# New prices for a planner that orders every engine, and one more wait

## The chip, the cores and the metric

The kernel runs on one core of a Trainium2 chip. The core has five engines that work side by side, each through its own list of instructions, and that meet only at semaphores: TensorE (PE, matrix products into PSUM), VectorE (DVE), ScalarE (ACT, here mostly exponentials), GpSimd (POOL) and SyncE (SP, which issues the DMAs). The metric is the time of one execution on the device in microseconds; of several runs the median is taken. "PEld" in the profile is TensorE's loading of weights.

## The reference

The inputs are x (2048 tokens of 512 values), wqkv (512 x 1536), wo (512 x 512), w_gate and w_up (512 x 1376), w_down (1376 x 512) and gate_w (512). Three things are computed and mixed:

```python
g = sigmoid((x * gate_w).sum(-1, keepdims=True))
# attention, 32 heads of 16
q, k, v = (x @ wqkv) split into heads
p = softmax(q @ k.T * 16 ** -0.5)
a = (p @ v) @ wo
# gated bilinear layer
b = ((x @ w_gate) * (x @ w_up)) @ w_down
return g * a + (1 - g) * b
```

The costly part is the softmax: 32 heads x 2048 x 2048 exponentials.

## The kernel before, in words

**Tiling.** The queries are cut into four chunks of 512 tokens (c), the heads into four groups of eight (b), and a group into two halves of four heads (p = 0, 1). One (c, b, p) is a stage m, of which there are 32. Inside a stage the keys are cut into 16 tiles of 128 (kt). A **unit** is one head of a stage with one key tile: scores of 128 keys x 512 queries, which fill one of the eight PSUM banks. There are 32 x 16 x 4 = 2048 units.

**What happens to a unit.** TensorE computes the scores (line 1224) as four small matmuls of 64 x 32 in one of its two row groups; the two row groups run side by side, and such a set of four is a *pack*. The exponential is then taken in one of two ways. ScalarE takes two neighbouring banks in one activation and writes two cells of PT (line 1319, a *pair*). Or VectorE takes one bank and forms the exponent's bits by an addition into int16 (line 1383, a *pass*); such a unit needs three further copies of its cell, shifted by a constant, which VectorE (line 1336) or GpSimd (line 1335) makes, and in the product with V all four cells are used, against four scaled copies of V. The product with V (PV, line 1669) is again made in packs, one for each row group, into one bank for the stage. A unit of ScalarE thus costs TensorE two PV matmuls (one in each row group), a unit of VectorE eight.

**The end of a stage.** The function `norm` handles it. VectorE copies the stage's bank to the raw buffer `oraw` (line 1608). DMAs then take the denominators out (`den`), VectorE forms the reciprocal (line 1543), further DMAs write it to memory and read it back spread over the partitions (`rb`), and GpSimd multiplies the raw output of both halves of a pair of stages by it (line 1586). For the second half, four DMAs first move its rows within `oraw`. `oraw` and `rb` are used again by the next pair of stages.

**Fills.** Between the scores and the PV packs TensorE works through a list of other products in packs (line 559): projections of q, k, v, the gate, the bilinear layer, and the output projection. VectorE empties their banks. The weights of the bilinear layer are loaded by SyncE into a ring of five slots.

**What sets the order.** Everything is ordered by a planner that runs when the program is built. It plays the five engines in time, each action with a price: `a_cad(n)` for a ScalarE activation of n banks, `d_cad` and `d_fast` for VectorE, `p_cad` for GpSimd, `PEC` = 0.2155 us for a pack and `PEL` = 0.437 us until its result is seen, and for each DMA a time to issue (the argument `cost`) and a time to land. `A_LAT`, `D_LAT`, `P_LAT` are the times until others see an end. Whenever an engine is free, its policy picks what it does next from what is ready in planned time: `pe_policy` tries a score first, then PV and fills in an order that depends on the stage. In `score`, a unit goes to ScalarE if its planned backlog is below 0.6 us (`TLO`), or up to 1.6 (`TA`) if VectorE can't take it, and to VectorE if VectorE's planned load is below 1.2 us, or 0.6 when a unit is already queued for it (`DTH`, `DTH2`), and if enough cells and a bank are free. ScalarE's units use banks 0 to 3, everything else banks 4 to 7. The order so found is written out for each engine with the semaphore waits that the data need. On the chip each engine then runs its list in that order as fast as its waits let it; the planned times play no further part.

Of the kernel before, what the change touches and what calls it, by code (L numbers as in the profile page):

```python
# [125 lines left out]

class _Res:

    __slots__ = ("at", "rel")

    def __init__(self):
        self.at = 0.0
# [51 lines left out]
def _build(nc, A_x, A_wqkv, A_wo, W_gate, W_up, W_down, gate_w, out):  # L184
# [10 lines left out]
    NB = 4  # L195
# [13 lines left out]
    NW = 5  # L209
# [42 lines left out]
    XC = 0.26  # L252
    AW = 0.3
    KF = 0
    GM = (2, 1)

    def a_cad(n):
        return 0.0505 + 0.4267 * n

    A_LAT = 0.17  # L260

    def d_cad(n):
        return 0.068 + n / 960.0
# [15 lines left out]
    with ExitStack() as stack:  # L279
# [56 lines left out]
        def at(t):  # L336
            heapq.heappush(events, t)

        def issue_pe(t, rgs, dur, lat, fn, deps, stream, own=()):
            o = P.op("pe", fn, deps, "pe", 1, own)  # L340
            o.tag = stream + ("" if len(rgs) == 2 else str(rgs[0]))
            if t < PH and stream != "pe_w":
                dur *= 2
            for r in rgs:
                free[f"pe{r}"] = t + dur
                busy[f"pe{r}"] += dur
            o.beg = t
            o.dur = dur * len(rgs) / 2
            o.vis = t + dur + lat
            at(t + dur)  # L350
            at(o.vis)
            return o

        def vis(deps):
# [297 lines left out]
        def q_half(n, p, src):  # L652
            hs = p
            if n == 0 and p == 0:
                return
            ops = []
            prev = 2 * n + p - NH
            for jj in range(2):
                for r in range(2):
                    a = 64 * r + 32 * jj + 16 * p  # L660
                    dma(
                        0,
                        QT[a : a + 16, hs, jj, :],
                        QR[a : a + 16, :],
                        lambda: src + [o_qz] + (h_last(prev) if prev >= 0 else []),
                        f"dq{hs}",
                        2.8,
                        ops.append,
                        0.6,
                    )  # L670
                    sq[-1].alt = lambda: prev < 0 or prev in q_last
            ev_q[n, p] = ops
# [170 lines left out]
        def load_w(c, f):  # L843
            n = c * FT + f
            w = FW[f]

            def prior():
                if f >= NW:
                    return [w_free.get((n - NW, 0)), w_free.get((n - NW, 1))]
                if c:  # L850
                    return [d_end.get((c - 1, tt)) for tt in range(4)]
                return [d_wv]

            for i, src in enumerate((W_up, W_gate)):
                dst = PT[:, c_w + 2 * (f % NW) + i, :].bitcast(BF16).rearrange("p (kt n) -> p kt n", kt=KD)

                def after(o, i=i):
                    w_slot[n, i] = o

                dma(  # L860
                    5 + 2 * n,
                    dst[:, :, 0:w],
                    src[:, f * 128 : f * 128 + w].rearrange("(kt p) n -> p kt n", p=128),
                    prior,
                    f"dwug{f % NW}_{i}",
                    3.5 if n >= NW else 4.6,
                    after,
                    0.42 if n >= NW else 0.6,
                )
                sq[-1].alt = lambda: None not in prior()  # L870

        def load_d(c):
            for s_ in range(NW + 1):
                f0, f1 = 2 * s_, min(2 * s_ + 2, FT)

                def prior(s_=s_):
                    if s_ == NW:
                        return [d_end.get((c - 1, tt)) for tt in range(4)] if c else [d_wv, o_dz]
                    last = max(f for f in range(FT) if f % NW == s_)
                    return [w_free.get((c * FT + last, 0)), w_free.get((c * FT + last, 1))]  # L880

                if s_ < NW:
                    dst = wd[:, f0:f1, :]
                    src = W_down[f0 * 128 : f1 * 128, :].rearrange("(f p) n -> p f n", p=128)
                else:
                    dst = wd[0 : FW[-1], FT - 1, :]
                    src = W_down[(FT - 1) * 128 : F, :]

                def after(o, s_=s_):
                    d_wd[c, s_] = o  # L890

                dma(6 + 2 * (c * FT + FT), dst, src, prior, f"dwd{s_}", 3.5, after)
                sq[-1].alt = lambda prior=prior: None not in prior()

        def mk_ug(c, f, i):
# [600 lines left out]
            return True  # L1496

        o_tail = {}

        def norm(m):  # L1500
            c, qd = divmod(m, NQ)
# [1 line left out]
            pair = c * NB + b  # L1503
            bank = obank[m]
            last = npv[m, "op"]
            prev = o_mult.get(divmod(pair - 1, NB)) if pair else None
            single = m == last_m - 1

            def after(o):
                release(banks[bank], [o])  # L1510
                o_tail["o", m] = o
                if p == 1:
                    o_tail["mv", m] = []
                    for j in range(4):
                        dma(
                            1,
                            oraw[32 * j + 16 : 32 * j + 32, 0, :],
                            oraw[32 * j + 16 : 32 * j + 32, 1, :],
                            lambda: [o, o_tail["o", m - 1], o_tail["den", m - 1]],
                            "dmv",  # L1520
                            2.9,
                            o_tail["mv", m].append,
                            0.6,
                        )
                row0 = 16 - p
                dma(
                    0,
                    den4[:, p, :],
                    oraw[row0:128:32, p, :].rearrange("j (a b) -> j a b", b=16),
                    lambda: [o],  # L1530
                    f"dden{p}",
                    3.2,
                    dened,
                    0.58,
                )

            def dened(o1):
# [9 lines left out]
            def reced(o2):  # L1547
                dma(
                    0,
                    scr[:, p, :].rearrange("j (a b) -> j a b", b=16),  # L1550
                    rec4[:, p, :],
                    lambda: [o2, o_tail.get(("rb", m - 2)), o_tail.get(("rb", m - 1)), o_tail.get(("rb", m - 3))],
                    f"drec{p}",
                    3.3,
                    scred,
                    0.55,
                )

            def scred(o3):
                o_tail["rec", m] = o3  # L1560
                if p == 1 or single:
                    scs = scr[:]
                    w = [o_tail["rec", m - i] for i in range(p + 1)]
                    if single:
                        for j in range(4):
                            bc = bass.AP(scs.tensor, scs.offset + 1024 * j, [[0, 16], [1, 512]])
                            dma(0, rb[32 * j : 32 * j + 16, :], bc, lambda: w + [prev, o_tail["rbz"]], "drb", 3.5, rbed if j == 3 else None)
                        return
                    mv = o_tail["mv", m]
                    bc = bass.AP(scs.tensor, scs.offset, [[512, 8], [0, 16], [1, 512]])  # L1570
                    dma(0, rb[:, :], bc, lambda: w + [prev, o_rbz], "drb", 4.8, lambda o: rbed(o, mv), 0.66)

            def rbed(o5, mv=()):
                o_tail["rb", m] = o5
# [23 lines left out]
            def zo(o):  # L1598
# [5 lines left out]
            dve_job(  # L1604
                0,
                d_cad(512),
                lambda: list(last) + [prev],
                lambda v: v.tensor_copy(oraw[:, p, :], ps[:, bank, :]),  # L1608
                after,
            )  # L1610
# [164 lines left out]
        def fill_go(t, r):  # L1775
            for f in active:
                n = len(f.packs)
                if f.wide:
                    pd = f.pd(f.pos) if f.pd else []
                    if vis(pd) > t:  # L1780
                        return False
                    if max(free["pe0"], free["pe1"]) <= t:
                        fill_issue(t, f, r, pd)
                    else:
                        st["hold"] = True
                    return True
                if (f.rg if f.pos < n else 1 - f.rg) == r and (f.pos != n or f.last.vis <= t):
                    fill_issue(t, f, r, [])
                    return True
            return False  # L1790

        def pv_go(t, r, part):
# [6 lines left out]
                return False  # L1799
            lead = pdone.get((m, r), 0) - pdone.get((m, 1 - r), 0)  # L1800
            if st["orow"] == (m, 1 - r):
                if olast_op[m, 1 - r].vis > t:
                    return False
                if lead > -PB and st["burst"] < PB and all(pv_ready(t, m, 1 - r)):
                    return False
            elif lead >= PL and all(pv_ready(t, m, 1 - r)):
                return False
# [189 lines left out]
```

## Time and profile before

| | |
|---|---|
| median of 3 runs | 717.59 us (715.14, 717.59, 719.7) |
| the profiled execution | 716.57 us, span 714.7 us |
| granted TensorE clock, mean | 0.999 |
| pairs on ScalarE (line 1319) | 747 |
| passes on VectorE (line 1383) | 554 |
| score, PV and fill matmuls (lines 1224, 1669, 559) | 8192, 7420, 5536 + 480 |
| DMAs | 34.86 MB, mean 49 GB/s |

2 x 747 + 554 = 2048: each unit is in one of the two rows. A row of the groups gives the line, engine and operation, what is written and read, the count, then the busy time in us and the mean length of one in ns, then the idle time of the engine before such instructions and who ended most of it. A row of the waits reads "who waited <- for whom: us in total, times, longest". A row of the timeline gives start, length, engine, line and count; neighbours of one kind are merged into a row as long as no idle time lies between them. A row of the windows gives the stretch, its length, the busy time with the number of instructions, the clock, and the share and rate of the DMAs.

### The profile page before, as it was taken

The page shows a single profiled execution, that of the slowest core. Times are in us where ns is not written, and L with a number is a line of the kernel's source. Part 1 is how long each engine was busy: PE and PEld are TensorE (multiplying, and loading weights), DVE is VectorE, ACT ScalarE, POOL GpSimd, SP SyncE. Part 2 cuts the span into 40 slices and gives each one's busy share as a digit, 9 for nine tenths or more (in the row PEclk, how much of TensorE's full clock was granted, in tenths as well). Part 3 has the DMA queues.
Part 4 walks back from the last instruction along what each step waited for, and adds up shares of the span by engine and source line. Part 5 has one row for each costly group of instructions (what it writes and reads, how often), then busy time and mean ns, then how long its engine had stood idle before and what let it go on. Part 6 is the DMA issues. An engine that isn't in the chain of part 4 may idle for free.

```text
span 714.7 us, 47027 instructions
## 1 busy us (share of the span) xinstructions
PE 704.0 (99%) x21790; PEld 382.6 (54%) x21794; DVE 661.6 (93%) x1367; ACT 696.2 (97%) x763; POOL 447.9 (63%) x487
## 2 busy tenths in 40 slices
PE   9999999999999999999999999999999999999997
PEld 5555555545555455555545555555555555565542
DVE  5779999999999989999999989999899998999995
ACT  6999999999999999999999999999999999999996
POOL 3116677666557557747756757777476776675771
PEclk9999999999999999999999999999999999999999
DMA  8300112111110232212110142122104222120101
GB/s 246 81 8 8 29 22 61 38 38 56 38 27 10 47 85 50 67 29 60 38 28 26 36 101 60 36 59 58 39 8 100 61 53 71 38 59 6 29 7 38
DMA packets 77619, 34.86 MB, mean 49 GB/s; under 512 B 60784, under 2 KB 74480, under 8 KB 77424
## 3 DMA queue, kind: packets, MB, share of 16 engines
q1 hardware_dynamic: 76624, 31.47, 17.9%
q8 instruction: 170, 2.79, 1.6%
q10 hardware_dynamic: 800, 0.39, 0.2%
q14 instruction: 25, 0.20, 0.1%
HBM read 25.23 MB, written 2.35 MB: 39 GB/s over the span
## 4 chain that ended last, share of the span: by engine, by line
PE 94%; ACT 2%; DVE 2%; issue 1%; DMA 0%; DVEq 0%
PE ps L1224 33%; PE ps L1669 32%; PE ps L559 27%; ACT PT L1319 2%; DVE PT L1383 1%; PE ps L593 1%; PE ps L555 1%; PE ps L502 1%; DMA den<-oraw 0%; PE ps L776 0%; DVE VV L750 0%; DVE PT L1336 0%; DVE ost L1957 0%; DVE VV L740 0%; DVE gden L832 0%
## 5 line engine op out<-in xcount | busy, mean ns | idle before, releaser
L1319 ACT ACTIVATE PT<-ps 128x1024 bf16<-128x1024 f32 x747 | 688.9, 1070 | 7.1 <-PE ps L1224 4.2
L1669 PE MATMUL ps<-PT,VV 64*32 64x512 bf16 x7420 | 552.9, 377 | 1.4 <-issue 0.8
L1335 POOL TENSOR_SCALAR PT<-PT 128x1024 int16<-128x1024 int16 (+1 forms) x450 | 417.4, 955 | 206.4 <-DVE PT L1336 144.7
L1224 PE MATMUL ps<-QT,KT 64*32 64x512 bf16 x8192 | 477.8, 379 | 0.4 <-issue 0.2
L559 PE MATMUL ps<-PT 64*32 64x512 bf16 x5536 | 400.3, 377 | 2.8 <-DVE PT L1383 1.8
L1383 DVE TENSOR_SCALAR PT<-ps 128x512 int16<-128x512 f32 x554 | 364.1, 683 | 23.0 <-PE ps L1224 16.5
L1669 PEld LDWEIGHTS ps<-PT,VV 64*32 64x32 bf16 x7420 | 189.2, 92 | 90.4 <-PE ps L1669 11.8
L1224 PEld LDWEIGHTS ps<-QT,KT 64*32 64x32 bf16 x8192 | 137.5, 89 | 163.0 <-ACT PT L1319 93.4
L1336 DVE TENSOR_SCALAR PT<-PT 128x1024 int16<-128x1024 int16 (+1 forms) x505 | 170.4, 397 | 0.3
L559 PEld LDWEIGHTS ps<-PT 64*32 64x32 bf16 x5536 | 137.5, 92 | 60.2 <-DVE PT L1383 9.1
L559 PE MATMUL ps<-wo,OT 64*32 64x512 bf16 x480 | 37.1, 377 | 0.0
L1586 POOL TENSOR_TENSOR OT<-oraw,rb 128x512 bf16<-128x512 f32 x16 | 20.5, 1282 | 20.6 <-DVE PT L1336 17.8
L925 DVE TENSOR_TENSOR PT<-ps,usb 128x512 bf16<-128x512 f32 (+1 forms) x44 | 30.0, 681 | 1.1 <-PE ps L559 1.1
L910 DVE CAST usb<-ps 128x512 bf16<-128x512 f32 (+1 forms) x44 | 29.8, 679 | 0.7 <-PE ps L559 0.6
L740 POOL TENSOR_SCALAR VV<-VV 128x528 bf16<-128x528 bf16 x12 | 7.6, 633 | 29.1 <-DVE VV L750 26.3
L1608 DVE COPY oraw<-ps 128x512 f32<-128x512 f32 x31 | 21.2, 683 | 0.9 <-PE ps L1669 0.7
L750 DVE CAST VV<-ps 128x512 bf16<-128x512 f32 x16 | 10.8, 688 | 8.1 <-PE ps L559 8.1
L559 PEld LDWEIGHTS ps<-wo,OT 64*32 64x32 bf16 x480 | 12.4, 91 | 5.4 <-DVE PT L1383 0.6
L634 DVE CAST KT<-ps 128x512 bf16<-128x512 f32 x16 | 10.9, 681 | 4.2 <-PE ps L555 2.4
L974 DVE TENSOR_SCALAR bsb<-ps,omg 128x512 bf16<-128x512 f32 x16 | 11.9, 742 | 0.2 <-PE ps L559 0.2
L618 DVE CAST PT<-ps 128x512 bf16<-128x512 f32 x14 | 9.0, 682 | 3.0 <-PE ps L593 3.0
L691 DVE TENSOR_SCALAR QR<-ps 128x512 bf16<-128x512 f32 x16 | 10.9, 681 | 0.0
(51 smaller groups left out, 80.0 us busy)
## 6 DMA issues: line engine op xcount, KB each, us to landing
PT<-in_B_w_up_dram SPq DMA_DIRECT2D x40, 128.0 KB, 3.2
PT<-in_B_w_gate_dram SPq DMA_DIRECT2D x40, 128.0 KB, 3.2
PT<-in_B_w_down_dram SPq DMA_DIRECT2D x20, 256.0 KB, 2.8
rb<-rscr SPq DMA_DIRECT2D x15, 256.0 KB
QT<-QR SPq DMA_DIRECT2D x124, 16.0 KB, 2.2
oraw<-oraw SPq DMA_DIRECT2D x60, 32.0 KB, 2.2
out_dram<-ost SPq DMA_DIRECT2D x14, 128.0 KB, 1.9
PT<-in_A_x_dram SPq DMA_DIRECT2D x3, 512.0 KB, 7.3
```

The costliest lines, as they stand in the source:

```text
L559: o = pe.matmul(ps[32 * i : min(w, 32 * i + 32), bank, :], lhs(32 * i, min(w, 32 * i + 32))[q], rhs[q], start=s0, stop=s1, tile_position=( ...
L910: lambda v: v.tensor_copy(usb[0:w, n % 2, :], ps[0:w, bank, :]),
L925: lambda v: v.tensor_tensor(hT[0:w, f, :], ps[0:w, bank, :], usb[0:w, n % 2, :], ALU.mult),
L974: lambda v: v.tensor_scalar(bsb[:, tt, :], ps[:, bank, :], omg[:, t : t + 1], None, ALU.mult),
L1224: o_ = pe.matmul(ps[32 * i_ : 32 * i_ + 32, x, :], KT[64 * r : 64 * r + 64, b, kt * 128 + 32 * i_ : kt * 128 + 32 * i_ + 32], QT[64 * r : ...
L1319: lambda a: a.activation(span(PT, cs).bitcast(BF16), span(ps, bs), ACT.Exp, scale=ESC),
L1335: return lambda e: e.tensor_scalar(span(PT, ds), span(PT, cs), 1.0, float(SH[k]), ALU.mult, ALU.add)
L1336: return lambda e: e.tensor_single_scalar(span(PT, ds), span(PT, cs), float(SH[k]), ALU.add)
L1383: lambda v: v.tensor_scalar(span(PT, cs), span(ps, bs), IOFF, 0.0, ALU.add, ALU.max),
L1586: lambda g: g.tensor_tensor(OT[:, pair % 6, :], oraw[:, 0, :], rb[:, :], ALU.mult),
L1608: lambda v: v.tensor_copy(oraw[:, p, :], ps[:, bank, :]),
L1669: o_ = pe.matmul(ps[32 * j : 32 * j + 32, ob, :], v_ap(k, kt, 8 * b + 2 * j + p, p)[rows], PT[rows, cell, :].bitcast(BF16), start=f0, stop ...
```

## The change

The planner's prices change; what is computed does not. ScalarE's activation of n banks is priced 0.0636 + 0.4267 n in place of 0.0505 + 0.4267 n, its latency 0.162 in place of 0.17. A new constant `OWN` of 0.02 us is added where TensorE must wait for its own last pack in the other row group. SyncE's times to issue are raised for most DMAs. And in `norm` the multiplication of the previous pair is looked up when the dependence is asked for, not when `norm` is called; if it is not planned yet, the copy to the raw buffer waits for it, where before it would have had no such wait.

```diff
     KF = 0
+    OWN = 0.02
 
     def a_cad(n):
-        return 0.0505 + 0.4267 * n
-    A_LAT = 0.17
+        return 0.0636 + 0.4267 * n
+    A_LAT = 0.162
...
 # issue_pe
             at(o.vis)
+            at(o.vis + OWN)
...
 # issue times: q_half, load_w, load_d (with its landing), and norm's dmv, dden, drec
-    0.6,
+    0.68,
...
-    0.42 if n >= NW else 0.6,
+    0.62 if n >= NW else 0.6,
...
-    dma(6 + 2 * (c * FT + FT), dst, src, prior, f"dwd{s_}", 3.5, after)
+    dma(6 + 2 * (c * FT + FT), dst, src, prior, f"dwd{s_}", 3.6, after, 0.5)
...
-    0.6,      # dmv
+    0.68,
-    0.58,     # dden
+    0.6,
-    0.55,     # drec
+    0.6,
...
+        never = _Res()
+        never.vis = INF
 
         def norm(m):
-            prev = o_mult.get(divmod(pair - 1, NB)) if pair else None
+            prev = lambda: [o_mult.get(divmod(pair - 1, NB), never)] if pair else []
...
             dve_job(
                 0,
                 d_cad(512),
-                lambda: list(last) + [prev],
+                lambda: list(last) + prev(),
                 lambda v: v.tensor_copy(oraw[:, p, :], ps[:, bank, :]),
...
 # fill_go
-                if (f.rg if f.pos < n else 1 - f.rg) == r and (f.pos != n or f.last.vis <= t):
+                if (f.rg if f.pos < n else 1 - f.rg) == r and (f.pos != n or f.last.vis + OWN <= t + 1e-9):
...
 # pv_go
-                if olast_op[m, 1 - r].vis > t:
+                if olast_op[m, 1 - r].vis + OWN > t + 1e-9:
                     return False
```

The two DMAs that read the reciprocals back (`drb`) take the same `prev()`.

More of the change, by code (lines that the diff above doesn't have):

```diff
@@ L127 @@
 class _Res:
-    __slots__ = ("at", "rel")
+    __slots__ = ("at", "rel", "vis")
     def __init__(self):
@@ L1566, in scred @@
                             bc = bass.AP(scs.tensor, scs.offset + 1024 * j, [[0, 16], [1, 512]])
-                            dma(0, rb[32 * j : 32 * j + 16, :], bc, lambda: w + [prev, o_tail["rbz"]], "drb", 3.5, rbed if j == 3 else None)
+                            dma(0, rb[32 * j : 32 * j + 16, :], bc, lambda: w + prev() + [o_tail.get("rbz", never)], "drb", 3.5, rbed if j == 3 else None)
                         return
@@ L1570, in scred @@
                     bc = bass.AP(scs.tensor, scs.offset, [[512, 8], [0, 16], [1, 512]])
-                    dma(0, rb[:, :], bc, lambda: w + [prev, o_rbz], "drb", 4.8, lambda o: rbed(o, mv), 0.66)
+                    dma(0, rb[:, :], bc, lambda: w + prev() + [o_rbz], "drb", 4.8, lambda o: rbed(o, mv), 0.66)
             def rbed(o5, mv=()):
```

## The prediction

> **What bounds the kernel now.** I read the page's engine totals first, then the chain that ended last, then the costliest groups, then who waits for whom.
>
> ```profile
> span 714.7 us, 47027 instructions
> PE 704.0 (99%) x21790; PEld 382.6 (54%) x21794; DVE 661.6 (93%) x1367; ACT 696.2 (97%) x763; POOL 447.9 (63%) x487
> PE 94%; ACT 2%; DVE 2%; issue 1%; DMA 0%; DVEq 0%
> L1319 ACT ACTIVATE PT<-ps 128x1024 bf16<-128x1024 f32 x747 | 688.9, 1070 | 7.1 <-PE ps L1224 4.2
> L1383 DVE TENSOR_SCALAR PT<-ps 128x512 int16<-128x512 f32 x554 | 364.1, 683 | 23.0 <-PE ps L1224 16.5
> ```
>
> Three engines look full, and the chain names TensorE with 94%. I do not take TensorE as the bound: matmuls are pipelined and overlap, so its 99% is not a rate. The trace lets me count it. There are 8192 + 7420 + 5536 + 480 small matmuls, four to a pack, and two row groups run side by side: 2703 packs for each group. Packs that follow each other closely in one row group start 0.22 us apart (418.14, 418.36 and 418.58 in the timeline), so the group needs 595 of 715 us, about 83%. The chain walks through TensorE because a score (L1224) and an activation hand a PSUM bank back and forth, as the list of waits shows:
>
> ```profile
> PEld ps L1224 <- ACT PT L1319: 93.4, 387, 0.6
> ACT PT L1319 <- PE ps L1224: 4.2, 9, 0.9
> DVE rec L1543 <- DMA den<-oraw: 1.4, 1, 1.4
> ```
>
> TensorE waits 93.4 us for ScalarE; ScalarE waits 4.2 us for the scores. So ScalarE's 747 pairs are the bound. Now their real price, from the timeline of ScalarE alone (start, length, how many):
>
> ```profile
> 20.11 4.69 ACT L1319 ACTIVATE PT<-ps 128x1024 bf16<-128x1024 f32 x5 [0.24 <-PE ps L1224]
> 148.97 21.24 ACT L1319 ACTIVATE PT<-ps 128x1024 bf16<-128x1024 f32 x23
> 419.45 1.02 ACT L1319 ACTIVATE PT<-ps 128x1024 bf16<-128x1024 f32 x1 [1.18 <-PE ps L559]
> ```
>
> One pair lasts 1.07 us but overlaps the next. Five undisturbed pairs give (4.69 - 1.07) / 4 = **0.905 us** from start to start. A long stretch without a visible hole gives (21.24 - 1.07) / 22 = **0.917**: an overlap of 0.16 us can be eaten by a late score before any idle time is shown. Over the whole kernel the first pair starts at 10.1 and the last at 704.2: 746 steps in 694.1 us, **0.930** each. Against 0.905 (675.1 us) the excess is 19.0 us. Small hidden waits are 746 x 0.012 = 9.0 of it. Visible holes are the rest, 10.0: 6.3 us of idle time inside the run (7.1 less 0.85 before the first pair) and 0.16 of lost overlap at each of some 22 holes.
>
> The old planner charged 0.0505 + 2 x 0.4267 = 0.904 for a pair, the undisturbed figure; the new one charges 0.917, the figure of a dense stretch. So neither is a mistake: one is what ScalarE can do, the other what it does in company.
>
> **The change, part by part.** No instruction is made shorter. Everything comes through the order that the planner writes.
>
> *ScalarE's price, 0.904 to 0.917.* The same 747 pairs cost 685.0 in the plan in place of 675.2, so 9.8 us more. The planner hands a unit to VectorE when ScalarE's planned backlog reaches 0.6 us and VectorE's planned load is low, so in a longer plan VectorE takes more units. At what rate, the windows of L1383 tell:
>
> ```profile
> 80.00:160.00 80.00, 45.74 (x70) 1.00 0.17 39
> 160.00:240.00 80.00, 47.72 (x73) 1.00 0.11 31
> 240.00:320.00 80.00, 42.35 (x65) 1.00 0.27 61
> ```
>
> Seven full windows hold 65 to 73 passes, 0.86 a us. If n pairs move, the plan is 9.8 - 0.917 n longer and VectorE takes 0.86 times that, which must be 2n: n = 3.0. So about 744 pairs and 560 passes, and ScalarE saves 3 x 0.917 = **2.75 us**. The six more passes cost VectorE 0.66 us each for the pass (364.1 / 554) and 0.31 for its share of the copies (L1336, 170.4 us), 5.8 us in all, beside some 53 that it is not busy. Each brings 6 more small PV matmuls (four cells in place of one, two row groups): 36 matmuls, 4.5 double packs, 1.0 us of TensorE, hidden by the 17% that it has free; without that cover the gain falls to 1.75. Ends for this part: no unit moves, 0; or VectorE takes all that its holes allow. Eight windows of 80 us from 40 to 680 leave it 32 us free, at 0.97 a unit 33 units or 16 pairs: 15 us. I take the rate, since it is what VectorE did with the same gates.
>
> A sentence apart: the Trainium skill's page "ScalarE: Activation LUTs", section "What ACT_TABLE_LOAD costs", gives an activation with immediate scale and bias 186 ns + 0.833 ns per element, with 93 ns of overlap back to back; for 1024 elements I estimate 0.946 us from it, by which even the new price is too low and the three pairs would be worth 2.84. The trace does not bear it out, since 746 x 0.946 = 705.7 us is longer than the 694.1 that the pairs really took.
>
> *What the small waits do (9.0 us).* If the order now has 0.012 us more room behind every pair, late scores may be caught up: down to 0, a gain of 9.0. Or the room is filled with another TensorE pack, which is a rival below. The rules that place the packs are the same and the latencies from score to ScalarE are not touched, so I count nothing.
>
> *SyncE's issue times.* Weight issues go from 0.42 to 0.62 and 0.4 to 0.5, the shuffles of Q and of the raw output from 0.6 to 0.68, the chain of the denominators by 0.02 to 0.05. One of the 22 holes comes from here, and it is the largest:
>
> ```profile
> 413.36 1.34 SPq L433 DMA_DIRECT2D PT<-in_B_w_gate_dram  x1
> 414.74 0.50 SPq L433 DMA_DIRECT2D PT<-in_B_w_down_dram  x1
> 415.29 0.61 SPq L433 DMA_DIRECT2D den<-oraw  x1
> 417.29 0.25 DVE L1543 RECIPROCAL rec<-den 128x16 f32<-128x16 f32 x1 [1.39 <-DMA den<-oraw]
> ```
>
> Five weight issues ran from 411.73 to 415.24, 3.5 us; four at 0.42 and one at 0.4 make 2.1 in the old plan, 3.0 in the new. The denominators were issued behind them, the reciprocal stood first in VectorE's queue, and ScalarE missed 1.18 + 0.16 = **1.3 us**. With the new prices the reciprocal is written further back, so I take this hole as gone; it is 0 if another 1.3 us issue falls elsewhere. Otherwise SyncE has room: of its queue only starts matter, and weights are loaded a slot ring ahead. What moves with the new prices are its own 411 issues, and they pass nothing but each other.
>
> *TensorE's own waits, 0.02.* A pack that must wait for the other row group's last pack into its bank is now planned 0.02 later. The list of waits has 39 such cases at L1669, 11.8 us; 39 x 0.02 = 0.8 at most, either way, off the bound. I take 0.
>
> *The missing wait.* The copy to the raw buffer (L1608) now always waits for the multiplication of the previous pair (L1586), even one not yet planned. In the trace that is always over:
>
> ```profile
> 386.34 1.28 POOL L1586 TENSOR_TENSOR OT<-oraw,rb 128x512 bf16<-128x512 f32 x1
> 389.09 0.69 DVE L1608 COPY oraw<-ps 128x512 f32<-128x512 f32 x1
> ```
>
> Here GpSimd ends at 387.62 and the copy starts 1.47 us later, which is the closest of the fifteen; the widest is 7.8. So it costs 0. If the cover went, the passes and copies behind it on VectorE would stand, then TensorE for their banks, then ScalarE: the reciprocal's 1.39 us became 1.18 of ScalarE's, so about 0.85 us per us late. Most would be the whole multiplication, 1.28 x 15 = 19; nothing suggests it.
>
> **The sum.** -2.75 - 1.3 = -4.1 us. The profiled execution took 716.57 (10.1 before the first pair, 694.1 of pairs, 10.5 from the last one's start to the end, 1.9 outside the span), so 712.5. The median of the runs shown, 717.59, is 1.0 above that execution; with the same distance I forecast **713.5**. The runs shown span 715.14 to 719.7, so about 1% is what can be told from no change.
>
> **The rivals.**
>
> *Room filled with another pack (slower).* A pair of 0.905 holds 0.905 / 0.22 = 4.11 packs of a row group, one of 0.917 holds 4.17. Once in some 18 pairs, 41 times, the planner can put one more pack ahead of a score, believing that the bank is not free yet. In truth the bank comes free 0.012 earlier, and the score stands behind 0.22 us of matmuls: 41 x 0.2 = 8.5 us lost. With the gain of 4.1 that is +4.4: 722; without it, 726. From 20 such places on it cancels my gain. For it: TensorE works in order and ScalarE's first releaser is L1224. Against: scores go first in the planner, and TensorE has 17% free. Chance 0.2.
>
> *Nothing moves.* The units stay as they are or the order is merely dealt anew, the hole at 419 returns elsewhere. For it: two visible holes (0.86 us before 258.31, 0.55 before 610.63) follow waits called "issue", which no price in the plan knows. 717 to 719. Chance 0.18.
>
> *Much more moves.* VectorE takes half of its free time, 8 pairs, and half of the small waits are caught up: -7.3 - 4.5 - 1.3 = -13: 704.5. For it: the page's waits show VectorE idle 16.5 us for scores alone. Against: copies and free cells limit the passes too. Chance 0.15.
>
> **Chances and range.** My forecast, 1 to 7 us faster, has 0.47. Below 710.4 (1% faster) lie nearly all of the third rival and a little of the forecast, 0.2; above 724.8 most of the first rival without its offsetting gain, and orders that lose more, 0.14; 0.66 between. From 706 to 724 no more than 2 in 10 is left out.
>
> **What would show it.** In the new profile: L1319 x742 to x745 and L1383 x558 to x564; the first pair still near 10; 0.925 to 0.93 from pair to pair; no hole over 1 us behind the reciprocal; no wait of L1608 for POOL. I am wrong if the number of pairs stays or rises, or if the mean step rises above 0.932 with more waits of ScalarE for L1224.

## The result and the profile after

The changed kernel takes **714.17 us** in the median of 20 runs (712.16 to 716.59), the kernel before 717.68 (715.14 to 719.7): a ratio of **0.9956**, 95% interval 0.9943 to 0.9969, or 3.2 us less by the ratio. The forecast was 713.5. The profiled execution took 715.41 us with a span of 713.6.

The page of the changed kernel, the lines that answer to those shown of before (the code is two to four lines longer here: L1319 is L1321, L1224 is L1226, L1669 is L1673, L1383 is L1385, L1543 is L1547, L1608 is L1612):

```profile
span 713.6 us, 47150 instructions
...
PE 702.9 (99%) x21826; PEld 388.1 (54%) x21830; DVE 667.4 (94%) x1398; ACT 696.5 (98%) x760; POOL 445.4 (62%) x489
...
L1321 ACT ACTIVATE PT<-ps 128x1024 bf16<-128x1024 f32 x744 | 689.3, 1056 | 7.3 <-PE ps L1226 4.8
...
L1385 DVE TENSOR_SCALAR PT<-ps 128x512 int16<-128x512 f32 x560 | 365.9, 683 | 16.9 <-PE ps L1226 9.0
...
L1612 DVE COPY oraw<-ps 128x512 f32<-128x512 f32 x31 | 21.1, 681 | 0.0
```

The counts are those of the forecast: 744 pairs and 560 passes. The copy to the raw buffer has no idle time before it, so on the chip the added wait never holds. But there are three pairs less and ScalarE's busy time is not shorter: 689.3 against 688.9. And the mean length of a pair fell from 1070 to 1056 ns, which looks like a gain and is none, because the recorded length includes the overlap with the forerunner: a pair that starts late is recorded as shorter. In the kernel before, pairs that started at most 0.91 us after their forerunner are recorded at 1.08 us in the mean, those that started 0.925 or more after it at 1.05; in the changed kernel it is 1.07 and 1.04, with more of the second kind (158 for 122). Why the first kind is recorded as shorter too is not shown. The list of waits (who waited for whom, us in total, times, longest):

```profile
PEld ps L1226 <- ACT PT L1321: 57.2, 258, 0.8
...
ACT PT L1321 <- PE ps L1226: 4.8, 10, 0.9
```

A score now waits for ScalarE's bank in 258 cases where it did in 387 (57.2 us for 93.4). More often than before, the bank is free already when the score comes: it is the score that is late.

**Where the time went.** I split the span by the starts of the pairs. The floor is 0.9045 us from start to start, the undisturbed step: 431 of the 746 steps of the first profile of before lie between 0.903 and 0.906. A *small late start* is a step of 0.925 to 1.07, of which only what is above 0.9045 is counted; a *larger* one is above 1.07. The rest are the time before the first pair, the time after the last one's start, and the 2.3 to 2.7 us by which steps below 0.925 exceed the floor, most of it in the steps of about 0.92 that follow a late start. The parts add up to the span by construction. Times in us; two executions of each kernel were profiled, the second together with the experiments.

| | before | after |
|---|---|---|
| first pair's start | 10.15, 9.41 | 9.14, 9.66 |
| floor | 674.8 | 672.0 |
| small late starts | 7.3, 8.0 | 10.5, 10.6 |
| larger ones | 9.3, 12.8 | 9.8, 9.5 |
| last pair's start to the end | 10.4, 10.4 | 9.8, 9.8 |

So, in the mean of two executions, the three pairs gave back 2.7 us, the small late starts took 2.9, the larger ones gave 1.4, the end 0.7, the start 0.4. Together that is 2.3 us less, and the profiled spans fell by 2.35 (714.7 and 717.6 to 713.6 and 714.0); the timed runs fell by 3.2.

### The profile page after: what moved, and what is told of

The parts are those of the page before. It is cut to its first block, busy times and chain, and to the rows that moved or that the text cites. A ratio compares the mean times of both kernels' runs of the same rounds, so it can differ in the third digit from the quotient of the medians.

```text
span 713.6 us, 47150 instructions
## 1 busy us (share of the span) xinstructions
PE 702.9 (99%) x21826; PEld 388.1 (54%) x21830; DVE 667.4 (94%) x1398; ACT 696.5 (98%) x760; POOL 445.4 (62%) x489
## 3 DMA queue, kind: packets, MB, share of 16 engines
HBM read 25.23 MB, written 2.35 MB: 39 GB/s over the span
## 4 chain that ended last, share of the span: by engine, by line
PE 87%; ACT 9%; DVE 1%; DMA 1%; SPq 1%; issue 0%; DVEq 0%
PE ps L1226 31%; PE ps L1673 30%; PE ps L561 26%; ACT PT L1321 8%; DMA gw<-in_gate_w_dram 1%; SPq L446 1%; DVE PT L1385 0%; DVE PT L1338 0%; PE ps L557 0%; PE ps L595 0%; DVE KT L636 0%; DVE ost L1961 0%; DVEq L104 0%; ACT KT L1930 0%; ACT KT L1931 0%
## 5 line engine op out<-in xcount | busy, mean ns | idle before, releaser
L1321 ACT ACTIVATE PT<-ps 128x1024 bf16<-128x1024 f32 x744 | 689.3, 1056 | 7.3 <-PE ps L1226 4.8
L1673 PE MATMUL ps<-PT,VV 64*32 64x512 bf16 x7456 | 559.4, 377 | 2.7 <-issue 1.6
L1226 PE MATMUL ps<-QT,KT 64*32 64x512 bf16 x8192 | 485.1, 379 | 1.2 <-ACT PT L1321 0.6
L1385 DVE TENSOR_SCALAR PT<-ps 128x512 int16<-128x512 f32 x560 | 365.9, 683 | 16.9 <-PE ps L1226 9.0
L1673 PEld LDWEIGHTS ps<-PT,VV 64*32 64x32 bf16 x7456 | 192.5, 92 | 101.5 <-PE ps L1673 10.1
L1226 PEld LDWEIGHTS ps<-QT,KT 64*32 64x32 bf16 x8192 | 140.7, 89 | 144.8 <-ACT PT L1321 57.2
L1338 DVE TENSOR_SCALAR PT<-PT 128x1024 int16<-128x1024 int16 (+1 forms) x530 | 178.1, 398 | 0.2
L561 PE MATMUL ps<-wo,OT 64*32 64x512 bf16 x480 | 34.8, 377 | 0.0
L1612 DVE COPY oraw<-ps 128x512 f32<-128x512 f32 x31 | 21.1, 681 | 0.0
```

The source lines that it names most:

```text
L561: o = pe.matmul(ps[32 * i : min(w, 32 * i + 32), bank, :], lhs(32 * i, min(w, 32 * i + 32))[q], rhs[q], start=s0, stop=s1, tile_position=( ...
L1226: o_ = pe.matmul(ps[32 * i_ : 32 * i_ + 32, x, :], KT[64 * r : 64 * r + 64, b, kt * 128 + 32 * i_ : kt * 128 + 32 * i_ + 32], QT[64 * r : ...
L1321: lambda a: a.activation(span(PT, cs).bitcast(BF16), span(ps, bs), ACT.Exp, scale=ESC),
L1338: return lambda e: e.tensor_single_scalar(span(PT, ds), span(PT, cs), float(SH[k]), ALU.add)
L1385: lambda v: v.tensor_scalar(span(PT, cs), span(ps, bs), IOFF, 0.0, ALU.add, ALU.max),
L1673: o_ = pe.matmul(ps[32 * j : 32 * j + 32, ob, :], v_ap(k, kt, 8 * b + 2 * j + p, p)[rows], PT[rows, cell, :].bitcast(BF16), start=f0, stop ...
```

## The experiments

All twelve were timed against the kernel before on their chip, in three groups of four. Ratios are to the kernel before, with 95% intervals. The edits are shown against the changed kernel or the one before, as said. The terms in the table below are those of the split above, from one profiled execution each.

| | pairs and single banks | floor | small | larger | end | ratio |
|---|---|---|---|---|---|---|
| before_again | 747 | 674.8 | 8.0 | 12.8 | 10.4 | 1.0012 (0.9994 to 1.0031) |
| hole_moved | 747 | 674.8 | 7.3 | 14.0 | 10.4 | 0.9977 (0.9964 to 0.9989) |
| price_0890 | 749 | 676.6 | 6.6 | 10.4 | 12.9 | 0.9988 (0.9975 to 1.0001) |
| others_only (0.904) | 748 | 674.8 | 8.1 | 7.8 | 11.1 | 0.9942 (0.9923 to 0.9961) |
| sync_only (0.904) | 747 | 673.9 | 7.5 | 8.5 | 13.2 | 0.9968 (0.9949 to 0.9986) |
| own_only (0.904) | 746 | 672.9 | 8.8 | 11.4 | 9.5 | 0.9962 (0.9949 to 0.9975) |
| old_price_744 (0.904) | 744 | 672.0 | 7.6 | 10.0 | 12.5 | 0.9945 (0.9925 to 0.9966) |
| old_price_gate (0.904) | 744 | 671.1 | 8.7 | 9.1 | 10.6 | 0.9938 (0.9921 to 0.9956) |
| price_only (0.917) | 744 | 672.0 | 11.3 | 10.0 | 9.5 | 0.9947 (0.9928 to 0.9966) |
| after_again (0.917) | 744 | 672.0 | 10.6 | 9.5 | 9.8 | 0.9959 (0.9940 to 0.9978) |
| new_price_741 (0.917) | 741 | 669.3 | 11.3 | 10.3 | 10.6 | 0.9918 (0.9895 to 0.9941) |
| price_0930 | 738 | 665.7 | 13.9 | 16.5 | 11.5 | 1.0019 (1.0006 to 1.0031) |

An activation of a single bank is counted with the pairs in the first column and left out of the floor. Five of the orders have one: in others_only, sync_only, old_price_gate and price_0930 it is the last activation and adds 0.9 to 1.1 us to the column of the end, in own_only it stands in the middle and adds 1.0 to the larger late starts.

**First group: is it the pairs, the room, or a new deal?** *price_only* keeps only ScalarE's price and latency (against the changed kernel; all of SyncE's issue times go back):

```diff
-    OWN = 0.02
+    OWN = 0.0
...
-    0.62 if n >= NW else 0.6,
+    0.42 if n >= NW else 0.6,
...
```

> The new price and latency of ScalarE alone; SyncE's issue times and TensorE's own wait as before. Its order holds 744 pairs and 560 passes. Theory of pairs (mine: a pair that leaves ScalarE is worth 0.92 us, the small waits stay): 3 pairs, 2.75 us faster than before, 714.9. Theory of room (the gain comes from the true price, which leaves late scores time to be caught up, whatever the pairs): nearly the whole 3.5 us, 714.2. Theory of a new deal (any new order falls within 3 us of the old one by chance): anything from 714 to 721.

*others_only* is the complement:

```diff
-        return 0.0636 + 0.4267 * n
-    A_LAT = 0.162
+        return 0.0505 + 0.4267 * n
+    A_LAT = 0.17
```

> The whole change but ScalarE's price and latency, which stay as before. Its order holds 748 pairs and 553 passes, one pair more than before. Theory of pairs: one pair, +0.9 us, less 1.3 if the hole behind the reciprocal goes: 717.3. Theory of room: no gain, 717.7. New deal: 714 to 721.

*old_price_744* takes the prices of before and opens VectorE's gate until it takes as many units as in the changed kernel; *new_price_741* opens the same gate in the changed kernel:

```diff
-    DTH2 = 0.6
+    DTH2 = 0.8
```

> All prices as before, but VectorE may have a queued unit up to a planned load of 0.8 in place of 0.6, so that the order holds 744 pairs and 560 passes, as many as the changed kernel. Theory of pairs: 2.75 us faster than before, 714.9. Theory of room: no gain, 717.7, since the price stays at 0.904. New deal: 714 to 721.

> The whole change, and the same gate of VectorE at 0.8: 741 pairs and 566 passes. Theory of pairs: three pairs less than the changed kernel, 2.75 us less than its 714.2, 711.4. Theory of room: as the changed kernel, 714.2. New deal: 711 to 718.

Measured, against 720.04 us of before on this chip: 715.83, 715.41, 715.58 and 714.24. ScalarE's price alone and everything but that price each give as much as the whole change (0.9947 and 0.9942 against 0.9956): the parts don't add up. My theory of pairs falls as the whole story, since others_only has 748 activations and is no slower than price_only with 744. It agrees as one term: between the changed kernel and new_price_741, at one price, three pairs less come with 0.38% less by the ratios, 2.7 us, and the small late starts hardly move. But new_price_741 is also another order, orders with nearly equal numbers of pairs differ by as much here, and its profiled span (713.7) is no shorter than those of the changed kernel; that the pairs alone made the 2.7 is not shown. The theory of room falls with old_price_744, which gains 0.55% at the old price. At 744 pairs each, old_price_744 and price_only take the same time: the new price costs 3.7 us more in small late starts, and the old-price order has an end that is 3.0 longer. That the order before was a slow one among its neighbours is what all four have in common.

**Second group: what is slow in the order before?** The kernel before against itself, the changed kernel again, and the two other parts alone (against the changed kernel, *sync_only* has `OWN = 0.0` and ScalarE's old price, *own_only* has SyncE's and ScalarE's old prices):

> The kernel before once more, timed against itself, for a second profile of it beside those of the others on one chip. Every theory expects no difference. What the profile is to tell is whether the small late starts of ScalarE (102 steps between 0.925 and 1.07 us, 7.3 us over 0.9045 in the first profile) and the hole behind the reciprocal at 419 come again: the theory that this hole belongs to the order expects it within 1 us of its place and at 1 us or more; the theory that it is an accident of one execution expects it gone.

> The changed kernel once more, for a second profile and a time beside the others. 3.5 us faster than before. If the new price fills the room behind a pair with TensorE's packs, the small late starts of ScalarE stay above 10 us (10.5 in the first profile); if they were an accident of one execution, they fall to the 7.3 of before.

> SyncE's issue times alone; ScalarE's price and TensorE's own wait as before. Its order holds 747 activations, one of them of a single bank, and 555 passes. Theory that SyncE's prices made the gain of the change without ScalarE's price: 4.6 us faster than before, as that one. Theory of pairs with the hole at 419: 1.3 to 1.8 us faster. Theory of a new deal (the order before is a slow one, and any neighbour is about 4 us faster): 2 to 6 us faster.

> TensorE's own wait of 0.02 us alone; the prices of ScalarE and SyncE as before. Its order holds 746 activations and 557 passes. Theory that SyncE's prices made the gain: no difference from before. Theory of pairs: 0.9 us faster. Theory of a new deal: 2 to 6 us faster.

before_again showed no difference, after_again 0.9959, sync_only 0.9968, own_only 0.9962. Each part alone, with 744 to 748 activations, takes 0.3 to 0.6% off. In the second execution of the kernel before, VectorE's and ScalarE's timelines at the old place of the hole:

```profile
414.90 0.74 DVE L1015 SCALAR_TENSOR_TENSOR ost<-ps,gval,bsb 128x512 bf16<-128x512 f32 x1
418.11 0.25 DVE L1543 RECIPROCAL rec<-den 128x16 f32<-128x16 f32 x1 [2.47 <-DMA den<-oraw]
```

```profile
409.58 8.43 ACT L1319 ACTIVATE PT<-ps 128x1024 bf16<-128x1024 f32 x9
420.28 4.69 ACT L1319 ACTIVATE PT<-ps 128x1024 bf16<-128x1024 f32 x5 [2.26 <-PE ps L559]
```

The hole came again, 1.18 us in the first execution and 2.26 in this one, so it belongs to the order. After the first 100 us four smaller holes also came in both, at the same places of the order: at 368 (0.40 and 0.54 us), 602 (0.41, 0.40), 611 (0.55, 0.45) and 623 (0.41, 0.41). In no other order did VectorE wait over 0.7 us for the denominators (old_price_744), and between 405 and 424 us ScalarE shows no hole over 0.5 in the other orders of these two groups; the changed kernel has three holes after the first 100 us that came in both of its executions (179, 266 and 568, of 0.46 to 0.56).

In the first profile of before, the copy to the raw buffer stands at

```profile
411.01 0.67 DVE L1608 COPY oraw<-ps 128x512 f32<-128x512 f32 x1
```

and in the changed kernel VectorE's and SyncE's timelines at that stage read:

```profile
408.55 0.68 DVE L1612 COPY oraw<-ps 128x512 f32<-128x512 f32 x1
...
413.77 0.24 DVE L1547 RECIPROCAL rec<-den 128x16 f32<-128x16 f32 x1
```

```profile
409.75 0.51 SPq L435 DMA_DIRECT2D PT<-in_B_w_up_dram  x1
410.31 0.61 SPq L435 DMA_DIRECT2D den<-oraw  x1
...
414.67 0.43 SPq L435 DMA_DIRECT2D PT<-in_B_w_gate_dram  x1
415.15 0.60 SPq L435 DMA_DIRECT2D rscr<-rec  x1
415.79 0.86 SPq L435 DMA_DIRECT2D PT<-in_B_w_down_dram  x1
```

The denominators are now issued ahead of two weight issues that used to stand before them, 1.1 us after the copy's end (408.55 + 0.68) in place of 3.6 (411.01 + 0.67 to 415.29), and the reciprocal starts at 413.77 with no wait. It is hardly further back on VectorE: ten instructions stand between the copy and it, where there were nine.

**Third group: the hole by itself, and the price in both directions.** *hole_moved* is the kernel before with that one reciprocal, and the DMA that needs it, put behind the next five VectorE instructions when the planner is done; everything else keeps its order:

```diff
             def reced(o2):
+                if m == 17:
+                    P.late = o2
...
+        at_ = P.ops.index(P.late)
+        later_ = [i for i, o in enumerate(P.ops) if i > at_ and o.eng == "dve"][:5]
...
         P.emit(nc, stack)
```

> The kernel before, order and prices untouched, but the one reciprocal that stood at 417 to 420 us waiting for its denominators is written behind the next five instructions of VectorE, together with the DMA that needs it. Theory that the hole is a loss of its own: ScalarE's hole of 1.2 to 2.3 us there goes, 1.3 to 2.4 us faster than before. Rival, that the hole hides other late work and is given back: no difference, and new holes within 20 us of the old place.

0.9977, that is 1.65 us (0.8 to 2.6) less. ScalarE's timeline of it runs through:

```profile
409.24 13.91 ACT L1319 ACTIVATE PT<-ps 128x1024 bf16<-128x1024 f32 x15
423.45 2.98 ACT L1319 ACTIVATE PT<-ps 128x1024 bf16<-128x1024 f32 x3 [0.29 <-PE ps L1224]
```

Of the hole 0.29 us is left, three us on. Its profiled execution took 721.14 us against a median of 718.69, with 14.0 us of larger late starts elsewhere, so its total is no measure; the timed runs are. This is the one part of the gain whose price was measured by itself.

*old_price_gate* (against the kernel before, with the missing wait) is the version that I had hoped to be the best by the three terms; *price_0930* and *price_0890* set the price of a pair to 0.930 and 0.890:

```diff
-    DTH = 1.2
+    DTH = 0.9                             # old_price_gate
-        return 0.0636 + 0.4267 * n
+        return 0.0766 + 0.4267 * n        # price_0930; price_0890 has 0.0365
```

> All prices as before; VectorE is offered a unit up to a planned load of 0.9 in place of 1.2. The order holds 744 activations and 561 passes and little work after the last pair. Three terms together: 3 pairs less 2.7, the holes of the old order gone 1.7 to 4, and none of the small late starts that the new price adds: 4.4 to 6.7 us faster than before. If the new price is what makes the gain: no difference.

> The whole change with ScalarE's pair priced at 0.930, the mean step that the first profile showed, in place of 0.917. The order holds 738 activations and 573 passes, six less than the changed kernel. Theory of pairs: 5.5 us faster than the changed kernel, 9 faster than before. Theory that a dear price lets TensorE put more packs ahead of the scores: scores wait for ScalarE's banks less than 57 us in all, the small late starts rise beyond 10.5 us by about 5.5, and the time stays within 1.5 us of the changed kernel.

> The whole change with ScalarE's pair priced at 0.890, less than ScalarE can do. The order holds 749 activations and 550 passes. Theory of pairs: 5 pairs more than the changed kernel, 4.6 us slower than it, 1 slower than before. Theory of the packs ahead: scores wait for ScalarE's banks 90 us or more, small late starts at 8 us or less, 2 us slower than the changed kernel.

old_price_gate came to 0.9938, 4.5 us less and at the low end of what I expected; its end is 10.6, not shorter as I had thought. price_0930 is slower than before although ScalarE has nine activations less, and some 4.5 us slower than the changed kernel by the ratios, where the theory of the packs had it within 1.5; so that theory got the direction of the waits and of the small late starts, and not the size of the whole. price_0890 is the same as before within its interval, and 0.3% behind the changed kernel, 2 us. These are the waits of the scores for ScalarE's banks at four prices. Price 0.890:

```profile
PEld ps L1226 <- ACT PT L1321: 126.8, 481, 0.8
```

Price 0.904, the profile of others_only:

```profile
PEld ps L1226 <- ACT PT L1321: 101.5, 431, 0.6
```

Price 0.917, of price_only:

```profile
PEld ps L1226 <- ACT PT L1321: 56.3, 266, 0.4
```

Price 0.930, its waits:

```profile
PEld ps L1226 <- ACT PT L1321: 33.7, 154, 1.3
```

And its row of ScalarE on the page:

```profile
L1321 ACT ACTIVATE PT<-ps 128x1024 bf16<-128x1024 f32 x738 | 689.5, 1034 | 12.8 <-PE ps L1226 5.9
```

The dearer a pair, the less often a score waits for its bank (481, 431, 266, 154), and the more small late starts ScalarE has (6.6, 8.1, 11.3, 13.9 us). The two in the middle also differ from the changed kernel in other prices; the changed kernel itself, at 0.917, has 258 such waits and 10.5 us. The same is seen in the time from the end of the pair that frees the banks to the start of the last score of the next pair in them: its median is 0.17 us at 0.890, 0.20 to 0.22 in the kernels at 0.904, 0.23 to 0.24 in those at 0.917, and 0.28 at 0.930; from 0.904 to 0.917 its lower quarter goes from 0.12 to 0.17. And it is packs that stand in between. The pairs in whose stretch from the freed bank to the last score TensorE starts at least four other matmuls (a pack's worth, of either row group) are 200 at 0.890, 256 to 295 at 0.904, 367 to 390 at 0.917 and 487 at 0.930. The number of pairs moved is not what does it: old_price_744 has 285 of them and 7.6 us of small late starts, new_price_741 has 390 and 11.3. At 0.930 all that ScalarE saves is lost: the floor falls by 6.3 against the changed kernel, the small late starts rise by 3.3, the larger by 6.9, the end by 1.7 (its single bank included). Why the larger ones rise was not followed.

The Trainium skill's page "ScalarE: Activation LUTs" (section "What ACT_TABLE_LOAD costs"), from which I had estimated 0.946 for a pair, would have asked for a price dearer still. The run at 0.930 shows that way to cost time here (1.0019, for 0.9956 at 0.917), and the trace has 0.9045 for the step.

The missing wait was not run alone: with the old prices the order written with it is the same, action for action, since each multiplication had been planned when it was asked for. With the new prices it is not. Written without the wait, the changed kernel's order differs near the end, from ScalarE's 737th action of 762 on: the last copy to the raw buffer is planned before the end of the multiplication that still reads that buffer, and no semaphore would hold it back. With the wait that copy is planned 1.2 us later, and the plan ends 1.1 us later. On the chip it follows closely:

```profile
689.47 1.28 POOL L1590 TENSOR_TENSOR OT<-oraw,rb 128x512 bf16<-128x512 f32 x1 [6.63 <-DVE PT L1338]
```

```profile
691.10 0.68 DVE L1612 COPY oraw<-ps 128x512 f32<-128x512 f32 x1
```

The copy starts 0.35 us after the multiplication's end (0.34 in the second execution), where the closest of before had 1.47. So the new prices need the wait, and what it costs in time was not measured.

## Why the prediction was right, and where it was not

- **The bound** was read rightly as far as the floor goes: ScalarE's pairs make 672 of 714 us. That TensorE has time to spare is only half right: the idle times that ScalarE shows in the changed kernel end with one of TensorE's matmuls in all cases but one, and at 0.930 the late starts cost more than nine pairs less save.
- **Three pairs move:** 744 and 560, as worked out from VectorE's rate; price_only has the same and others_only does not, so it is ScalarE's price with its latency that moves them. That it fits to the pair is partly luck: the same working gives three pairs more for the step to 0.930, and the order has six activations less. Their 2.75 us are in the floor (2.7), which is their number times the step. At one price, an order with three further pairs less was 2.7 us faster by the ratios (new_price_741).
- **The small waits, "I count nothing":** this is the step that failed. They rose by 2.9 us (7.3 and 8.0 to 10.5 and 10.6) and ate the pairs. It is my slower rival, room filled with another pack, at a third of its price of 8.5. The places are more than its 41 (269 and 286 pairs with a pack's worth of matmuls ahead of the score became 368 and 367, some 90 more), and each costs about 0.03 us in the mean (2.9 / 90) in place of 0.2. I had given it 0.2 as a whole case, where it was a term of the sum: it rises with the price in every run. "Scores go first in the planner" was no argument, because the planner puts a pack ahead of a score that is not yet possible in planned time and already is on the chip. My own sign of being wrong came with it: the mean step rose to 0.935 (0.9350 and 0.9348), above the 0.932 that I had set, with 10 waits of ScalarE for scores (4.8 us, in the second execution 3.2) for 9 (4.2). As a sign it was badly chosen, since the second execution of the kernel before has 0.9354 and 12 waits (5.2) itself.
- **The hole at the reciprocal, -1.3:** right in size, it measured 1.65 by itself (0.8 to 2.6), but it did not go the way I named. The reciprocal was not written further back to speak of; the denominators were issued ahead of two of the weights. And the hole also went in each part alone, own_only included, which does not touch SyncE's prices: any new order had a good chance to lose it. That it went was partly luck.
- **Left out of the sum:** the end, 0.7 us shorter, and other larger holes of the old order. The terms seen give -2.7 + 2.9 - 1.65 - 0.7 = -2.2 against -3.2 measured by the ratio; the remaining 1.0 is within what the larger late starts of one order vary from one execution to the next (9.3 and 12.8), and I can't put it down to a cause.
- **The added wait and TensorE's own waits:** the first shows no idle time, as said, but it is not always over by 1.47 us: it decides the order of the last stage, and its margin there is 0.35. For the second the list shows 33 waits at L1673 for its own packs, 10.1 us, for 39 and 11.8; own_only has 35 and 11.7. That `OWN` alone gave 0.38% I put down to another order with another set of holes, not to 39 x 0.02.

So the forecast of -4.1 stood near the result partly by luck: a term that I had at nothing, +2.9, was offset by 0.35 at the hole, 0.7 at the end and 1.0 without a known cause. Of "nothing moves" one half was true: "the order is merely dealt anew" describes a good part of the gain.

**A better version.** new_price_741, the changed kernel with VectorE's second gate at 0.8, beats both: 714.24 us against 720.04 of before in its group, 0.9918 (0.9895 to 0.9941), where the changed kernel has 0.9956 (0.9943 to 0.9969) and 0.9959; the first two intervals just part. The two were not timed in one group, and the interval of the changed kernel's repetition overlaps. Nothing of the computation changes in it.

## What to carry to other kernels

A price in a planner is not only a forecast of an engine's time: a price above what the engine can do at its best lets the planner place work of others in a room that is not there, and that work then stands ahead of the bound engine's input. Here that cost was 2.9 us, and in the total it was hidden by what else the order changed. Before a change of prices is credited, run each part alone and an unrelated nudge of the order: here each gave most of the gain or all of it, and the order that they were measured against had a hole of its own that was worth half of it and went in all of them. And when pairs overlap, a shorter mean length of an instruction can go with more late starts: 1091, 1070, 1056 and 1034 ns in price_0890, the kernel before, the changed kernel and price_0930.

## What was not expected of the hardware

- The time to issue a DMA on SyncE is not one number: in the kernel before 43 of 411 issues took over 1 us in one execution and 46 in the other, 26 of them the same ones; in the changed kernel 35 and 43, 21 the same. The median of a weight issue is 0.51. A single price, 0.42 or 0.62, fits neither kind. In both executions of the kernel before, one of the weight issues between the copy and the denominators was a slow one (1.34 and 1.53 us).
- One order's larger late starts differ by 3.5 us between two executions (9.3 and 12.8), and the first pair's start lay between 9.1 and 10.2 us over all profiles: a difference of 1 us between two profiled executions says little.
